# Keys 0 to 383 by threes in 128 partitions, a separate tile of tails, one k and one v load per pair of heads, six score buffers, a new order

## The chip, the cores and the metric

The kernel runs on one core of a Trainium2 chip. The metric is the device time of one execution in microseconds; the profile is of one execution of its own. The engines are TensorE (PE; PEld is its weight load), VectorE (DVE), ScalarE (ACT), GpSimd (POOL) and SyncE (SP), which issues most transfers. ACT issues some as well, in line with its calculations.

## The reference

Attention with mixed heads, for 4 batches, 12 heads, 448 positions and 64 values per head, then a gated network over the 768 joined values:

```
scores = (q @ k.T) / 8;  scores = sum over h of scores[h] * w_pre[h, g]
e = exp(scores - rowmax); a = e / (sum(e) + 1e-9)
a = sum over h of a[h] * w_post[h, g];  x = a @ v          (heads side by side)
h = relu(x @ w_in); c = 3-tap convolution of h along the positions
out = (h * sigmoid(c)) @ w_out
```

## The kernel before

A batch's 448 query rows are cut into four chunks, so there are 16 chunks c of 100 to 120 rows. Chunk c runs through these steps. `k_load`/`k_tr`/`k_out` and `q_load`/`q_tr`/`q_out` bring keys and queries and turn them on PE (tiles `tk`, `tq`; `pre` holds batch 0's keys, `nkr` later ones), `qk` makes the scores of two heads (tile `s`), and `qk_out` copies each head to a score buffer (`st`, or `stx` and `pre` at the start). `relayout` is a transfer of one head from its rows into `mt`, where ten query rows and twelve heads share the partitions, so that `premix` (tile `m`) mixes heads by one matmul. `premix` of a chunk needs all twelve re-layouts of it. Then `row_max` (VectorE), `row_exp` (ScalarE), the sums, and `postmix`, which mixes heads again and turns the result into two accumulators `t`; `post_out` copies them to `at`, one on ScalarE and one on VectorE, and only then can the next pair of tiles use them. `av` multiplies by v (tile `a`), `av_out` and `av_add` write x on ScalarE and VectorE.

The network is interleaved. Its weights come as 64-bit numbers and are decoded: `dec_load` (tile `raw`, two buffers), then five `dec_step`s, of which the first is ScalarE's (L354). `mm1` makes h, which goes out and comes back with a border for `conv`, `gate`, `glu`, and `mm2` makes the output rows.

Nothing is scheduled at run time. Each engine runs its instructions in the order in which the program emits them, and that order is the table `PLACES`: for each kind of step a list of places in one common order, which `plan` sorts. Transfers issued by SP stand in SP's queue in that order as well; a transfer that has to wait holds those behind it. Ahead of the plan, `FIRST` lists the first loads, alternately on SP and ACT.

The keys are not kept in their natural order along the 448 columns; any order does, as long as v has the same. Here partition j below 64 holds four neighbouring keys and partition j from 64 on holds three (JC = 4, TAIL = 64). So a pair of heads needs four k transfers (two per head: 64 partitions with four keys, 64 with three and a shared neighbour), and three v transfers (the four-key half, the three-key half, and a copy of each fourth key into the second half, so that both halves of the array have it). In batch 0 the two heads lie apart, with 1 KB per partition and head, and each key block is turned by one matmul per head.

Of the kernel before, what the change touches and what calls it, by code (L numbers as in the profile page):

```python
# [9 lines left out]
F32 = mybir.dt.float32  # L10
# [13 lines left out]
B, H, S, D = 4, 12, 448, 64  # L24
# [4 lines left out]
JC = 4  # L29
TAIL = 64  # L30
# [13 lines left out]
ST_X, ST = 12, 5  # L44
# [4 lines left out]
FIRST = [("q_load", 0, 0), ("k_load", 0, 0, 0), ("k_load", 0, 1, 0), ("k_load", 0, 2, 0), ("q_load", 0, 1), ("k_load", 0, 3, 0),  # L49
         ("k_load", 0, 4, 0), ("k_load", 0, 5, 0), ("q_load", 1, 0), ("q_load", 1, 1)]  # L50
# [8 lines left out]
def ring_slot(i):  # L59

    if i < 4 * H:
# [20 lines left out]
    qk_out=[14, 16, 28, 22, 23, 18, 37, 34, 40, 42, 49, 54, 53, 64, 58, 57, 63, 62, 68, 69, 74, 73, 127, 129, 137, 138,  # L82
# [9 lines left out]
    premix=[75, 80, 89, 93, 112, 166, 172, 181, 203, 205, 215, 306, 311, 325, 346, 348, 366, 418, 434, 444, 475, 495,  # L92
# [789 lines left out]
```

## Time and profile before

| | |
|---|---|
| three runs, median (lowest to highest) | 637.31 us (634.23 to 641.98) |
| the profiled execution, its own time | 641.89 us |
| its span, first to last instruction | 640.1 us |
| granted TensorE clock, mean | 0.981 |
| PE busy, weight loads busy | 592.9 us (93%), 477.2 us (75%) |
| VectorE, ScalarE, GpSimd busy | 439.1, 401.2, 78.0 us |
| transfers | 98.37 MB, mean 154 GB/s |

The attention of the 16 chunks ends at about 489 us, with the network's first product beside it; the rest is the network alone. A share of busy time is a mean over both.

### The profile page before, as it was taken

Reading aid. Unit: us, or ns where it says so; the run is one execution under the profiler, and the core shown is the slowest. Engines: PE = TensorE matmul, PEld = TensorE weight load, DVE = VectorE, ACT = ScalarE, POOL = GpSimd, SP = SyncE. Lnnn points to the kernel's source line nnn. Section 1 sums busy time; section 2 is a strip of 40 time slices with the busy share of each in tenths; the row PEclk is TensorE's granted clock in tenths of the full one; section 3 lists DMA queues with packets and bytes.
Section 4 is the critical chain, followed back from the end, with each engine's and each line's share of the span. In section 5 each row is a group of like instructions: output and inputs, shape, how many; then the busy total and the mean of one; then the engine's idle time right before and its main releaser. Section 6 shows DMA issues by size and latency. Waiting matters only on the chain.

```text
span 640.1 us, 26197 instructions
## 1 busy us (share of the span) xinstructions
PE 592.9 (93%) x11113; PEld 477.2 (75%) x11113; DVE 439.1 (69%) x1172; ACT 401.2 (63%) x1082; POOL 78.0 (12%) x165
## 2 busy tenths in 40 slices
PE   6987799999799999889999999999978999999997
PEld 4455676676667777667776876768768999999997
DVE  2564486687767678477666686857877999876721
ACT  1485686787678687687767688768757754232310
POOL 8001010011122112010111101121100000000000
PEclk8997998999989999999999999999997999999999
DMA  7565664776566665564566566555543324333211
GB/s 180 163 186 164 187 185 109 214 183 177 157 189 188 183 184 164 170 173 137 168 186 183 168 173 212 167 167 157 167 150 92 112 59 149 106 90 120 80 75 74
DMA packets 106708, 98.37 MB, mean 154 GB/s; under 512 B 56940, under 2 KB 97760, under 8 KB 106592
## 3 DMA queue, kind: packets, MB, share of 16 engines
q1 hardware_dynamic: 103628, 94.18, 50.8%
q10 hardware_dynamic: 2868, 2.52, 1.4%
q8 instruction: 87, 1.43, 0.9%
q14 instruction: 29, 0.24, 0.1%
q0 software_dynamic: 96, 0.01, 0.0%
HBM read 41.98 MB, written 15.99 MB: 91 GB/s over the span
## 4 chain that ended last, share of the span: by engine, by line
PE 70%; DMA 9%; issue 6%; DVE 5%; ACT 4%; SPq 3%; ACTq 1%; POOL 1%; POOLq 0%
PE o L816 18%; PE h L724 14%; PE m L543 9%; PE a L643 9%; PE t L587 8%; PE s L507 8%; DMA mt<-st 2%; DMA raw<-in_moe_w_in_dram 2%; DVE nm L548 2%; PE tq L484 1%; PE tk L463 1%; DMA v<-in_v_dram 1%; DMA raw<-in_moe_w_out_dram 1%; DMA pre<-in_k_dram 1%; DVE at L372 1%
## 5 line engine op out<-in xcount | busy, mean ns | idle before, releaser
L587 PEld LDWEIGHTS t<-wn,e 60*64 60x64 f32 x5040 | 104.4, 135 | 44.6 <-issue 28.4
L724 PE MATMUL h<-xp,lp 128*128 128x448 f32 x576 | 132.5, 377 | 5.4 <-ACT x L653 3.7
L556 ACT ACTIVATE e<-m,nm 124x448 f32<-124x448 f32 x180 | 113.7, 637 | 35.3 <-DVE nm L548 28.7
L548 DVE TENSOR_REDUCE nm<-m 124x1 f32<-124x448 f32 x180 | 106.6, 618 | 30.7 <-PE m L543 28.7
L724 PEld LDWEIGHTS h<-xp,lp 128*128 128x128 f32 x576 | 105.0, 189 | 23.2 <-ACT x L653 5.3
L816 PE MATMUL o<-wo,g 128*128 128x384 f32 x672 | 118.9, 337 | 0.0
L587 PE MATMUL t<-wn,e 60*64 60x60 f32 x5040 | 108.4, 221 | 10.7 <-issue 6.9
L816 PEld LDWEIGHTS o<-wo,g 128*128 128x128 f32 x672 | 117.7, 188 | 0.3
L543 PE MATMUL m<-mt,wpre 64*64 64x448 f32 (+1 forms) x704 | 91.9, 559 | 11.5 <-DMA v<-in_v_dram 4.8
L370 ACT COPY st<-s 120x448 f32<-120x448 f32 (+2 forms) x154 | 78.9, 543 | 30.5 <-DMA mt<-st 15.7
L507 PE MATMUL s<-mk,mq 64*64 64x448 f32 (+3 forms) x768 | 94.0, 547 | 2.6 <-ACT mk L370 2.5
L643 PEld LDWEIGHTS a<-at,v 64*64 64x64 f32 x3072 | 79.2, 138 | 22.3 <-issue 12.2
L643 PE MATMUL a<-at,v 64*64 64x120 f32 (+5 forms) x3072 | 85.5, 254 | 7.3 <-issue 3.4
L372 DVE COPY at<-t 128x420 f32<-128x420 f32 (+2 forms) x96 | 54.3, 565 | 37.9 <-PE t L587 34.6
L714 DVE TENSOR_TENSOR lp<-wi,lp 128x128 fp32r<-128x128 f32 x192 | 51.9, 289 | 20.7 <-ACT lp L710 20.5
L710 ACT CAST lp<-wi 128x128 fp32r<-128x128 f32 x192 | 54.7, 305 | 8.8 <-PE h L724 8.5
L562 POOL TENSOR_SCALAR sm<-sm 124x2 f32<-124x2 f32 (+1 forms) x92 | 22.5, 245 | 299.8 <-ACT e L556 279.0
L370 ACT COPY at<-t 128x420 f32<-128x420 f32 (+2 forms) x96 | 51.6, 543 | 9.7 <-PE t L587 9.2
L543 PEld LDWEIGHTS m<-mt,wpre 64*64 64x64 f32 (+1 forms) x704 | 30.2, 135 | 31.8 <-issue 17.4
L356 POOL TENSOR_SCALAR dw<-dw 128x256 f32<-128x256 f32 x48 | 41.4, 864 | 97.1 <-ACT dw L354 91.2
L507 PEld LDWEIGHTS s<-mk,mq 64*64 64x64 f32 (+3 forms) x768 | 29.5, 127 | 21.9 <-issue 10.8
L785 DVE SCALAR_TENSOR_TENSOR cv<-hpad,cws,cv 128x448 f32<-128x448 f32 x64 | 42.5, 680 | 1.0
(71 smaller groups left out, 501.1 us busy)
## 6 DMA issues: line engine op xcount, KB each, us to landing
mt<-st SPq DMA_DIRECT2D x82, 210.0 KB
h<-hs SPq DMA_DIRECT2D x32, 224.0 KB
hpad<-h SPq DMA_DIRECT2D x32, 224.0 KB
mt<-st SPq DMA_DIRECT2D x36, 192.5 KB
mt<-st SPq DMA_DIRECT2D x36, 175.0 KB
raw<-in_moe_w_in_dram SPq DMA_DIRECT2D x24, 256.0 KB
raw<-in_moe_w_out_dram SPq DMA_DIRECT2D x24, 256.0 KB
nqr<-in_q_dram SPq DMA_DIRECT2D x31, 192.0 KB
```

Of the source, the lines that this page charges most:

```text
L370: nc.scalar.copy(out=out, in_=in_)
L372: nc.vector.tensor_copy(out=out, in_=in_)
L507: nc.tensor.matmul(out=pqs[c, h - 1 + i][m:e], lhsT=qops[c][s, p, o + m:o + e], rhs=kops[b, p][s], start=True, stop=True)
L543: nc.tensor.matmul(out=pms[c, some[i]][64 * s:64 * s + 64], lhsT=wpre[rows, i], rhs=mt[rows, some[s]], start=True, stop=True)
L548: nc.vector.tensor_reduce(out=nm[0:PN], in_=pms[c, t][0:PN], axis=AX.X, op=ALU.max, negate=True)
L556: nc.scalar.activation(out=e[0:PN], in_=pms.pop((c, t))[0:PN], func=AF.Exp, bias=nm[0:PN], accum_out=sums[c, t // 2][0:PN, t % 2:t % 2 + 1])
L587: nc.tensor.matmul(out=pts[c, k][s][64 * half:64 * half + 64, block], lhsT=e[rows, o:o + 64], rhs=wn[rows, i], start=True, stop=True)
L643: nc.tensor.matmul(out=out, lhsT=vts[b, p][rows, hh, (j + 1) % JC], rhs=rhs, start=(j == 3 and p % 3 == 0), stop=(j == 2), skip_group_chec ...
L710: nc.scalar.copy(out=lps[b, f, kk][:, 0], in_=wi[:, kk, f * 128:(f + 1) * 128])
L714: nc.vector.tensor_tensor(out=t[:, 1], in0=wi[:, kk, f * 128:(f + 1) * 128], in1=t[:, 0].bitcast(F32), op=ALU.subtract)
L724: nc.tensor.matmul(out=phs[b, f], lhsT=w, rhs=x, start=(kk + j == 0), stop=(kk == KC - 1 and j == 2))
L816: nc.tensor.matmul(out=pos[r, o], lhsT=g, rhs=w, start=(f == 0 and j == 0), stop=(f == FC - 1 and j == 2))
```

## The change

Keys 0 to 383 lie by threes in 128 partitions (JC = 3, JM = 384). The 64 tails, keys 384 to 447, lie in a tile of their own: for k one of 64 partitions by 6 heads in each half (`kt`, one buffer), for v one with all twelve heads in both halves (`vtail`). `k_load` and `load_v` are one transfer per pair of heads; `k_tail` and `v_tail` are two per batch. `k_tr` is four transposes per pair in every batch, of which the first turns the tails of pairs p and p + 3 (its other half is overwritten). In batch 0 a key is now a piece of 256 bytes on both sides, as before in the others. A score pool has six buffers instead of five.

```
-JC = 4
-TAIL = 64
+JC, JM = 3, 384
-ST_X, ST = 12, 5
+ST_X, ST = 12, 6
-FIRST = [("q_load", 0, 0), ("k_load", 0, 0, 0), ("k_load", 0, 1, 0), ("k_load", 0, 2, 0), ("q_load", 0, 1), ("k_load", 0, 3, 0),
-         ("k_load", 0, 4, 0), ("k_load", 0, 5, 0), ("q_load", 1, 0), ("q_load", 1, 1)]
+FIRST = [("q_load", 0, 0), ("k_tail", 0, 0), ("k_load", 0, 0), ("k_tail", 0, 1), ("k_load", 0, 1), ("k_load", 0, 2), ("q_load", 0, 1),
+         ("k_load", 0, 3), ("k_load", 0, 4), ("k_load", 0, 5), ("q_load", 1, 0), ("q_load", 1, 1)]
...
+    v_tail=[148, 161, 753, 754, 1492, 1459, 2205, 2295],
...
+    kt_p = pool("kt", 1)
...
-    def k_load(b, p, hh, eng=nc.sync):
...
-        for h in (0, 1) if b == 0 else (hh,):
-            first = k[b, 2 * p + h]
-            eng.dma_start(out=x[0:TAIL, h], in_=first[0:JC * TAIL].rearrange("(j c) d -> j c d", c=JC))
-            rows = bass.AP(first.tensor, first[JC * TAIL - 1].offset, [[(JC - 1) * D, 128 - TAIL], [1, JC * D]])
-            eng.dma_start(out=x[TAIL:128, h], in_=rows.rearrange("j (c d) -> j c d", c=JC))
+    def tails_of(x, b, h0, h1):
+
+        return x[b, h0:h1, JM:S].rearrange("h j d -> j h d")
+
+    def k_load(b, p, eng=nc.sync):
+
+        nat["k", b, p] = nat["k0"][:, p] if b == 0 else nk_p.tile([128, JC, 2, D], F32, tag="nk", name="nkr")
+        eng.dma_start(out=nat["k", b, p], in_=k[b, 2 * p:2 * p + 2, 0:JM].rearrange("h (j c) d -> j c h d", c=JC))
+
+    def k_tail(b, i, eng=nc.sync):
+
+        if i == 0:
+            nat["kt", b] = kt_p.tile([128, H // 2, D], F32, tag="kt", name="kt")
+        eng.dma_start(out=nat["kt", b][64 * i:64 * i + 64], in_=tails_of(k, b, 6 * i, 6 * i + 6))
 
     def k_tr(b, p):
+
         pl, tag = (ps_m, "m") if b else (ps_t, "t") if p % 3 < 2 else (ps_a, "a")
-        trs["k", b, p] = pl.tile([128, JC, 128], F32, tag=tag, name="tk")
-        x = nat.pop(("k", b, p))
+        trs["k", b, p] = to = pl.tile([128, 512], F32, tag=tag, name="tk")
+        x, q, o = nat.pop(("k", b, p)), p % 3, JM - 64 * (p // 3)
+        nc.tensor.transpose(out=to[:, o:o + 128], in_=nat["kt", b][:, 2 * q:2 * q + 2].rearrange("j h d -> j (h d)"),
+                            identity=ident)
         for c in range(JC):
-            to = trs["k", b, p][:, (c - 1) % JC]
-            if b:
-                nc.tensor.transpose(out=to, in_=x[:, :, c].rearrange("j h d -> j (h d)"), identity=ident)
-                continue
-            for hh in range(2):
-                nc.tensor.matmul(out=to[64 * hh:64 * hh + 64], lhsT=x[:, hh, c], rhs=ident, start=True, stop=True)
+            nc.tensor.transpose(out=to[:, 128 * c:128 * c + 128], in_=x[:, c].rearrange("j h d -> j (h d)"), identity=ident)
...
     def load_v(b, p):
-        vts[b, p] = vall[:, p]
-        x = v[b, 2 * p:2 * p + 2]
-        lo = x[:, 0:JC * TAIL].rearrange("h (j c) d -> j h c d", c=JC)
-        nc.sync.dma_start(out=vts[b, p][0:TAIL].rearrange("j h c d -> j h (c d)"),
-                          in_=lo.rearrange("j h c d -> j h (c d)"))
-        nc.sync.dma_start(out=vts[b, p][TAIL:128, :, 1:JC].rearrange("j h c d -> j h (c d)"),
-                          in_=x[:, JC * TAIL:S].rearrange("h (j c) d -> j h (c d)", c=JC - 1))
-        nc.sync.dma_start(out=vts[b, p][TAIL:128, :, 0], in_=lo[:, :, 0])
+
+        nc.sync.dma_start(out=vmain[:, p].rearrange("j h c d -> j h (c d)"), in_=v[b, 2 * p:2 * p + 2, 0:JM].rearrange("h (j c) d -> j h (c d)", c=JC))
+
+    def v_tail(b, i):
+
+        nc.sync.dma_start(out=vtail[64 * i:64 * i + 64], in_=tails_of(v, b, 0, H))
...
-                    nc.tensor.matmul(out=out, lhsT=vts[b, p][rows, hh, (j + 1) % JC], rhs=rhs, start=(j == 3 and p % 3 == 0),
-                                     stop=(j == 2), skip_group_check=True)
+                    nc.tensor.matmul(out=out, lhsT=v_j, rhs=rhs, start=(j == JC and p % 3 == 0),
+                                     stop=(j == JC - 1), skip_group_check=True)
```

`postmix`, `post_out` and `av` are written for the new constants, with the same shapes. All of `PLACES` is new, for the network's steps too. Some of its places, and the PE steps that stand in the list between the two:

| the last `relayout` of a chunk, its first `premix` | before | after |
|---|---|---|
| chunk 1 | 165, 166: none | 133, 171: 1 premix, 4 postmix, 2 qk |
| chunk 3 | 400, 418: 1 qk, 2 postmix | 390, 425: 6 postmix, 1 k_tr, 3 qk |
| chunk 13 | 2278, 2280: none | 2253, 2294: 2 mm1, 2 qk, 2 postmix |
| chunk 14 | 2487, 2489: none | 2475, 2500: 3 postmix, 3 av, 2 qk |
| chunk 15 | 2599, 2635: 4 postmix, 2 premix, 3 av | 2652, 2653: none |

The later `v_tail` of batch 2 has place 1492, the last `av` of batch 1 has 1455 and the first of batch 2 has 1525, with four postmix and two premix between the last two. The last store of the output is of row group 12, in one transfer; it was of group 13, in two halves.

## Rows read from the trace of the kernel before

**Rows 1.** The page: busy time by engine; the chain that ended last.

```profile
PE 592.9 (93%) x11113; PEld 477.2 (75%) x11113; DVE 439.1 (69%) x1172; ACT 401.2 (63%) x1082; POOL 78.0 (12%) x165
...
PE 70%; DMA 9%; issue 6%; DVE 5%; ACT 4%; SPq 3%; ACTq 1%; POOL 1%; POOLq 0%
```

**Rows 2.** Windows: stretch, length, busy by engine, clock, DMA share, GB/s.

```profile
20.00:40.00 20.00, 18.57 (x252) 8.35 (x244) 13.90 (x32) 12.09 (x31) 0.81 (x4) 1.00 0.63 185
...
520.00:560.00 40.00, 40.00 (x226) 39.49 (x225) 36.33 (x72) 16.06 (x35) 0.00 (x0) 1.00 0.36 113
```

**Rows 3.** Timeline, 0 to 16 us: start, length, engine, line, operation [idle before].

```profile
0.81 0.61 ACTq L452 DMA_DIRECT2D pre<-in_k_dram  x1
...
5.66 0.59 SPq L478 DMA_DIRECT2D nqr<-in_q_dram  x1
...
9.16 0.90 PE L484 MATMUL tq<-ident,nqr 128*128 128x128 f32 x3 [3.49 <-DMA nqr<-in_q_dram]
...
12.94 1.28 ACT L414 ACT_TABLE_LOAD   x1 [12.94 <-DMA pre<-in_k_dram]
...
15.29 2.58 PE L507 MATMUL s<-mk,mq 64*64 64x448 f32 x24 [1.39 <-ACT mk L370]
```

**Rows 4.** Timeline, 42 to 54 us.

```profile
42.99 3.53 SPq L523 DMA_DIRECT2D mt<-stx  x4
...
46.57 0.97 SPq L617 DMA_DIRECT2D v<-in_v_dram  x1
...
51.58 3.27 PE L543 MATMUL m<-mt,wpre 64*64 64x448 f32 x16 [4.83 <-DMA v<-in_v_dram]
```

**Rows 5.** Timeline of PE alone, 90 to 460 us: the waits spoken of.

```profile
97.48 1.76 PE L543 MATMUL m<-mt,wpre 64*64 64x448 f32 x8 [1.66 <-DMA nkr<-in_k_dram]
...
176.44 1.49 PE L724 MATMUL h<-xp,lp 128*128 128x448 f32 x3 [3.72 <-ACT x L653]
...
398.46 0.98 PE L543 MATMUL m<-mt,wpre 64*64 64x448 f32 x8 [1.11 <-DMA mt<-st]
...
453.10 1.74 PE L543 MATMUL m<-mt,wpre 64*64 64x448 f32 x16 [0.79 <-DMA mt<-st]
```

**Rows 6.** Timeline, 163 to 178 us: SP's queue and ScalarE.

```profile
163.68 1.47 SPq L617 DMA_DIRECT2D v<-in_v_dram  x1
...
167.15 1.40 SPq L454 DMA_DIRECT2D nkr<-in_k_dram  x1
...
171.09 0.45 SPq L692 DMA_DIRECT2D raw<-in_moe_w_in_dram  x1
...
175.61 0.43 ACT L354 ACTIVATE dw<-raw 128x256 f32<-128x256 f32 x1 [1.96 <-DMA raw<-in_moe_w_in_dram]
```

**Rows 7.** Windows at the lower clock, columns as in rows 2.

```profile
51.50:56.50 5.00, 4.92 (x68) 3.08 (x72) 2.73 (x7) 2.23 (x7) 0.21 (x1) 0.50 0.58 166
97.00:101.00 4.00, 3.52 (x37) 1.77 (x41) 1.16 (x2) 0.96 (x3) 0.00 (x0) 0.57 0.67 177
176.00:180.00 4.00, 3.56 (x16) 2.93 (x20) 1.40 (x6) 2.50 (x8) 1.07 (x2) 0.57 0.72 235
```

**Rows 8.** One line's instructions, L452: duration in ns, least, median, most.

```profile
L452 SPq DMA_DIRECT2D nkr<-in_k_dram x36: 544/602/1767, 12.2 to 345.1; - x36
```

**Rows 9.** Groups by line and shape: turning keys of batches 1 to 3.

```profile
L463 PE MATMUL tk<-ident,nkr 128*128 128x128 f32 x72 | 11.2, 278 | 0.2
```

**Rows 10.** Timeline, 0 to 32 us: turning one pair of batch 0.

```profile
22.62 1.09 PE L466 MATMUL tk<-ident,pre 128*64 128x128 f32 x16
```

**Rows 11.** The chain in order of time: start, length, what.

```profile
2.09 3.39 DMA pre<-in_k_dram
...
92.11 5.31 DMA nkr<-in_k_dram
```

**Rows 12.** Timeline of PE alone, 30 to 480 us: two waits ahead of postmix.

```profile
40.27 1.08 PE L587 MATMUL t<-wn,e 60*64 60x60 f32 x55 [0.18 <-ACT at L370]
...
473.77 0.85 PE L587 MATMUL t<-wn,e 60*64 60x60 f32 x42 [2.25 <-issue]
```

More of the change, by code (lines that the diff above doesn't have):

```diff
@@ L264 @@
[L264 to L265 removed]
+    q_tr=[0, 9, 38, 59, 80, 92, 76, 198, 387, 463, 516, 560, 555, 588, 895, 886, 1010, 960, 1243, 1227, 1237, 1231,
+        1627, 1721, 1844, 1912, 2044, 1997, 2241, 2193, 2439, 2501],
+    q_load=[4, 19, 18, 149, 274, 430, 452, 494, 482, 499, 793, 808, 813, 941, 1087, 1165, 961, 1097, 1330, 1560, 1670,
+        1863, 1743, 1807, 2078, 2136, 1951, 2265],
+    k_tr=[5, 6, 2, 14, 36, 20, 327, 324, 395, 443, 466, 515, 735, 924, 1005, 1125, 1175, 1182, 1553, 1724, 1856, 1858,
+        1926, 2037],
@@ new lines @@
+    k_load=[243, 8, 366, 397, 432, 462, 677, 794, 963, 954, 1127, 1149, 1242, 1360, 1569, 1728, 1862, 1880],
+    k_tail=[233, 248, 573, 668, 1255, 1298],
+    v_tail=[148, 161, 753, 754, 1492, 1459, 2205, 2295],
+    qk=[11, 12, 31, 26, 44, 40, 48, 61, 68, 65, 78, 73, 82, 90, 85, 120, 146, 160, 245, 262, 282, 286, 297, 304, 416,
[4 rows of a table added]
+    qk_out=[17, 23, 46, 13, 33, 32, 29, 27, 45, 49, 41, 42, 57, 51, 66, 62, 69, 70, 67, 72, 79, 88, 75, 74, 83, 95, 91,
[9 rows of a table added]
+    premix=[96, 100, 114, 135, 130, 171, 175, 197, 221, 241, 209, 306, 315, 338, 341, 369, 388, 425, 440, 457, 489,
[4 rows of a table added]
@@ new lines @@
+    row_max=[97, 98, 101, 102, 117, 116, 138, 136, 131, 164, 172, 176, 193, 205, 208, 214, 222, 224, 255, 254, 210,
[9 rows of a table added]
+    sum_eps=[109, 112, 137, 166, 177, 185, 217, 232, 238, 278, 279, 321, 330, 364, 375, 410, 411, 455, 447, 510, 519,
[4 rows of a table added]
+    postmix=[119, 126, 140, 141, 155, 156, 173, 174, 183, 187, 211, 215, 226, 227, 251, 258, 275, 276, 292, 294, 301,
[9 rows of a table added]
+    post_out=[127, 128, 142, 147, 163, 168, 179, 178, 192, 196, 223, 216, 242, 234, 260, 271, 277, 281, 295, 299, 303,
[9 rows of a table added]
+    av=[230, 231, 256, 267, 268, 269, 314, 318, 320, 345, 351, 352, 448, 449, 467, 508, 533, 534, 591, 592, 593, 614,
[4 rows of a table added]
@@ new lines @@
+    av_out=[257, 272, 333, 353, 468, 535, 602, 617, 836, 873, 1080, 1102, 1271, 1301, 1415, 1458, 1535, 1619, 1824,
+        1881, 2065, 2094, 2123, 2167, 2425, 2488, 2589, 2625, 2748, 2763, 2789, 2809],
+    av_add=[261, 293, 336, 361, 484, 536, 605, 620, 837, 928, 1093, 1108, 1279, 1332, 1419, 1486, 1576, 1620, 1828,
+        1882, 2080, 2095, 2140, 2169, 2426, 2489, 2599, 2630, 2786, 2792, 2795, 2810],
+    load_cw=[514, 566, 746],
+    emit_cw=[790],
+    net_init=[2573],
+    room=[213],
+    dec_load=[16, 200, 244, 354, 402, 470, 547, 633, 597, 752, 806, 839, 911, 952, 984, 1008, 1047, 1067, 1119, 1147,
+        1198, 1190, 1267, 1305, 1337, 1354, 1416, 1454, 1558, 1636, 1600, 1731, 1667, 1779, 1840, 1886, 1913, 1986,
+        2003, 2165, 2131, 2272, 2264, 2334, 2395, 2421, 2493, 2495],
@@ new lines @@
+    relu=[728, 815, 938, 1023, 1161, 1239, 1369, 1517, 1578, 1693, 1732, 1794, 1855, 1948, 2015, 2051, 2225, 2296,
+        2347, 2405, 2474, 2531, 2695, 2732, 2894, 2890, 2922, 2972, 2956, 3048, 3041, 3135],
+    conv=[2650, 2651, 2697, 2723, 2784, 2791, 2729, 2754, 2774, 2839, 2852, 2853, 2862, 2863, 2885, 2913, 2914, 2927,
[5 rows of a table added]
+    wo_load=[2659, 2660, 2661, 2745, 2750, 2817, 2891, 2935],
+    mm2=[2944, 3012, 2987, 3042, 2967, 3038, 2943, 3045, 3058, 3059, 3046, 3060, 3071, 3134, 3072, 3151, 3122, 3129,
+        3108, 3127, 3168, 3169, 3214, 3244, 3163, 3164, 3159, 3166, 3193, 3275, 3270, 3289, 3233, 3261, 3266, 3267,
+        3189, 3265, 3242, 3243, 3276, 3278, 3286, 3287, 3283, 3285, 3293, 3295, 3284, 3288, 3307, 3309, 3271, 3300,
+        3303, 3304],
@@ new lines @@
+    mm2_out=[3013, 3043, 3139, 3140, 3084, 3085, 3175, 3192, 3144, 3150, 3202, 3245, 3204, 3205, 3298, 3299, 3263,
+        3268, 3279, 3280, 3282, 3291, 3294, 3296, 3308, 3310, 3301, 3305],
+    store=[3044, 3170, 3113, 3201, 3180, 3256, 3290, 3302, 3269, 3281, 3292, 3297, 3311, 3306],
+    q_out=[1, 25, 39, 60, 81, 93, 77, 199, 398, 464, 517, 576, 561, 589, 906, 892, 1011, 970, 1245, 1240, 1244, 1233,
+        1637, 1741, 1853, 1943, 2071, 2013, 2269, 2209, 2462, 2502],
+    k_out=[7, 10, 3, 15, 37, 21, 329, 326, 400, 450, 471, 518, 743, 935, 1016, 1148, 1176, 1183, 1561, 1738, 1867,
+        1860, 1928, 2053],
@@ L266 @@
+    wo_hi=[2692, 2727, 2782, 2751, 2804, 2854, 2983, 2954],
+    wo_lo=[2721, 2728, 2790, 2772, 2988, 2883, 3001, 2978],
 )
@@ L276, in indices @@
     some = dict(
-        q_tr=grid(NCH, 2), q_load=grid(range(2, NCH), 2), k_tr=grid(B, NP), k_load=grid(range(1, B), NP, 2),
+        q_tr=grid(NCH, 2), q_load=grid(range(2, NCH), 2), k_tr=grid(B, NP), k_load=grid(range(1, B), NP), k_tail=grid(range(1, B), 2), v_tail=grid(B, 2),
         qk=grid(NCH, range(1, H, 2)), qk_out=grid(NCH, H), premix=pairs, row_max=tiles, sum_eps=pairs,
@@ L435, in keep_busy @@
             nc.tensor.matmul(out=ps, lhsT=zero[:, 0:128], rhs=zero[:, 0:S], start=True, stop=True)
-    def keys(x, h):
-        lo, hi = x[h, 0:JC * TAIL], x[h, JC * TAIL:S]
-        return lo.rearrange("(j c) d -> j c d", c=JC), hi.rearrange("(j c) d -> j c d", c=JC - 1)
-    def k_load(b, p, hh, eng=nc.sync):
-        if ("k", b, p) not in nat:
-            nat["k", b, p] = (nat["k0"][:, p] if b == 0 else
-                              nk_p.tile([128, JC, 2, D], F32, tag="nk", name="nkr").rearrange("j c h d -> j h c d"))
-        x = nat["k", b, p]
-        for h in (0, 1) if b == 0 else (hh,):
-            first = k[b, 2 * p + h]
-            eng.dma_start(out=x[0:TAIL, h], in_=first[0:JC * TAIL].rearrange("(j c) d -> j c d", c=JC))
-            rows = bass.AP(first.tensor, first[JC * TAIL - 1].offset, [[(JC - 1) * D, 128 - TAIL], [1, JC * D]])
-            eng.dma_start(out=x[TAIL:128, h], in_=rows.rearrange("j (c d) -> j c d", c=JC))
+    def tails_of(x, b, h0, h1):
+        return x[b, h0:h1, JM:S].rearrange("h j d -> j h d")
@@ L468, in k_out @@
     def k_out(b, p):
         kops[b, p] = ko[:, (NP * b + p) % 7]
-        copy_of(("ACT", "DVE")[p % 2], kops[b, p], trs.pop(("k", b, p)).rearrange("p c j -> p (c j)")[:, 0:S])
+        copy_of(("ACT", "DVE")[p % 2], kops[b, p], trs.pop(("k", b, p))[:, 0:S])
     def q_load(c, g, eng=nc.sync):
@@ L577, in postmix @@
         if i == 0:
-            pts[c, k] = [ps_t.tile([128, 2 * JC - 1, 60], F32, tag="t", name="t") for s in range(2)]
+            pts[c, k] = [ps_t.tile([128, 2 * JC + 1, 60], F32, tag="t", name="t") for s in range(2)]
         e, wn = es.pop((c, 2 * k + i)), wns[c, k]
-        pieces = [(3 * i + j, half, 128 * j + 64 * half) for j in range(JC - 1) for half in range(2)]
-        pieces.insert(6 * i, (2 * JC - 2, i, S - TAIL))
+        pieces = [(3 * i + j, half, 128 * j + 64 * half) for j in range(JC) for half in range(2)]
+        pieces.insert(6 * i, (2 * JC, i, JM))
         for block, half, o in pieces:
@@ L584, in postmix @@
                 rows = slice(64 * s, 64 * s + 12 * HR)
-                if o == S - TAIL and len(PAIRS[c][k]) == 1:
+                if o == JM and len(PAIRS[c][k]) == 1:
                     half = s
@@ L595, in post_out @@
         if not ats:
-            ats["all"] = at_p.tile([128, 2 * JC - 1, 12, 90], F32, tag="at", name="at")
+            ats["all"] = at_p.tile([128, 2 * JC + 1, 12, 90], F32, tag="at", name="at")
         pair = len(PAIRS[c][k]) == 2
@@ L628, in av @@
             pas[c] = [pl.tile([128, 3, 128], F32, tag=tag, name="a") for pl, tag in ((ps_a, "a"), (ps_m, "m"))]
-        for j in (3, 0, 1, 2):
+        for j in (JC, 0, 1, 2):
             for hh in range(2):
                 for i in range(2):
-                    blocks = slice(j, j + JC, JC - 1) if j < 3 else slice(6, 7)
+                    blocks = slice(j, j + JC + 1, JC) if j < JC else slice(2 * JC, 2 * JC + 1)
                     rows = slice(64 * i, 64 * i + 64)
@@ L635, in av @@
                     out = pas[c][i][64 * hh:64 * hh + 64, p % 3].rearrange("d (b x) -> d b x", b=2)
-                    if j == 3:
+                    v_j = vmain[rows, p, hh, j] if j < JC else vtail[rows, 2 * p + hh]
+                    if j == JC:
                         out = out[:, i:i + 1]
@@ L831, in tile_talking_heads_conv_glu @@
     emit = {f.__name__: f for f in (
-        k_load, k_tr, k_out, q_load, q_tr, q_out, qk, qk_out, relayout, premix, row_max,
-        row_exp, sum_eps, sum_rec, post_w, postmix, post_out, load_v, av, av_out, av_add, x_hi, x_lo, w_hi, w_lo, load_cw, emit_cw,
+        k_load, k_tail, k_tr, k_out, q_load, q_tr, q_out, qk, qk_out, relayout, premix, row_max,
+        row_exp, sum_eps, sum_rec, post_w, postmix, post_out, load_v, v_tail, av, av_out, av_add, x_hi, x_lo, w_hi, w_lo, load_cw, emit_cw,
         dec_load, dec_step, dec_store, mm1, relu, store_h, wo_load, wo_hi, wo_lo, net_init, room, load_h, conv, gate,
```

110 lines of the change are left out of this document (34 added, 76 removed), and 250 rows, old and new, of tables (av, conv, dec_step, mm1).

## The prediction

> **What bounds the kernel now.** I read the page's busy times and the chain of waits first [rows 1]: TensorE (PE) is busy for 592.9 of 640.1 us and the chain runs through it for 70%, with 9% in transfers. So time can go only where PE stands idle (47.2 us in all), where its clock is halved, or where it has less to do. The windows say where not to look: from 520 us on PE is full, 40.00 of 40 us [rows 2]. The order is new there too, but PE has no idle time to give back, and I count nothing there but the last store. What is left is the start and the attention stage.
>
> The timeline of the start shows the largest single loss. The first score matmul begins at 15.29 us, 14 us after the first load was issued [rows 3]. Two things hold it. The second half of q, the sixth load in SP's list, is issued at 5.66 and frees PE at 9.16. And ScalarE, which has to copy the first transposed keys, is busy as an issuer: 17 loads stand ahead of its first calculation, which starts at 12.94. The second loss is at 46.75 us, where PE stops for 4.83 us ahead of the first premix of chunk 1 [rows 4]. The trace names a v load, but this matmul reads no v: it reads the re-laid scores, whose last four transfers SP issued up to 46.52, and 5.1 us later PE goes on. Such waits come back, shorter, at 97.48, 398.46 and 453.10, all ahead of the first premix of a chunk (3, 13 and 15), and 3.72 us at 176.44 [rows 5]. That last one is indirect [rows 6]: SP issues v and k loads from 163.68 and a weight piece only at 171.09; ScalarE stands at the decode of that piece until 175.61, and its copy of x, which PE waits for, is queued behind. After each of the longer stops the granted clock is at the lower level, 0.50 for 51.5 to 56.5 us [rows 7].
>
> **What the change does, part by part.** *Issues.* The list of loads falls from 96 for k and 72 for v to 32 and 32, tails included: 104 fewer on SP and ACT, at 0.602 us of queue each [rows 8] 63 us of queue time. SP isn't on the path as such, so this is worth nothing by itself; it counts where PE waits for something that SP issued late.
>
> *The start.* ACT now has six loads ahead of its first calculation instead of 17. At the 0.71 us each of before ((12.94 - 0.81)/17, [rows 3]) it is free at about 5.1 us and, after the 1.28 us of table load, at 6.4. The second half of q is SP's fourth load, not its sixth. So the first score matmul can come at 8 to 10 us. Keys of batch 0 are turned by four transposes per pair (0.156 us each, 11.2/72, [rows 9]) instead of a group of 1.09 us [rows 10]: 0.47 us less for each of six pairs, 2.8 us of PE work. If nothing else held PE, it would be at the premix of chunk 1 at 46.75 - 6.3 (start at 9.0) - 1.8 (three transposes and the list's difference) = 38.7 us instead of 51.58, a gain of 12.9. But the data have to come. Ahead of the last re-layout of chunk 1 the list of before moves 8.64 MB (counted from the tiles: q 1.38, k 1.70, decode 0.52, v 0.52, scores 4.52), that of after 7.92 MB. At the pace of before (8.64 MB by 51.58 us, 168 GB/s) they are there at 47.3 us; at the 185 GB/s of 20 to 40 us [rows 2] at 42.8 and the landing after it. I take 44.5, a gain of 7.1, less 0.7 us because the new list has done less other PE work there (one score group and one q turn more, four half postmixes fewer): **-6.4**, between -12.2 and -3.6.
>
> Batch 0's keys came in pieces of 1 KB and now come in pieces of 256 bytes, as the later batches' do: those landed in 5.31 us, the first ones in 3.39 [rows 11]. The Trainium skill ("DMA: Bandwidth & Descriptors", Why small descriptors are slow) speaks against this part: a 256-byte piece takes 11 cycles of which 8 carry data, by the same count a 1 KB one 35 of which 32 do, so a byte takes a quarter longer. By an estimate from that page 1.38 MB, 7.4 us at 185 GB/s, would take 1.9 us longer and this part would give -4.5.
>
> *The clock behind the stop.* 5.0 us at half clock cost 2.5 us of work [rows 7]. Whether PE stops long enough again is open: **-1.0** (-2.5 to 0).
>
> *Waits for re-laid scores.* From the last re-layout in the list to the first premix the old list has no PE work at all for chunks 1, 13 and 14, and 2.0 us for chunk 3; the new one has 4.9, 4.2, 5.6 and 6.5 (PE steps between the two places, at their durations in the timeline). The waits of chunks 3 and 13, 1.66 and 1.11 us, and the 4 us at clock 0.57 behind the first of them, 1.7 us [rows 5, 7], make 4.5: **-3.0** (-4.5 to 0).
>
> *ScalarE behind weight pieces.* 3.72 us and 1.7 us of clock [rows 5, 7]. In the new list one of 48 pieces has its decode step less than 1 us of PE work behind its load, in the old one eight; and in the stretch above three v and two k issues, of up to 1.47 us, stand ahead of the late piece [rows 6], where the new form has one of each. **-3.2** (-5.4 to 0).
>
> *What is new and costs.* (a) Chunk 15's last re-layout now stands directly ahead of its premix; it had 6.1 us. That distance cost chunk 14 nothing, chunk 13 1.11 and chunk 1 4.83 us: +1.0 (0 to 7.3 with the clock). (b) One v tail serves all heads, so it waits for the last value matmul of a batch, and the next batch's first one waits for it; SP's later loads are queued behind that wait. The tightest is batch 2's, with 4.0 us of PE work between, against 0.6 to issue and 5.31 to land: +0.8 (0 to 3.6). k tails have 9 us or more. (c) Both accumulators of postmix are taken by a pair of tiles, and nine hand-overs from pair to pair now have under 1 us of PE work between, in the old list two. At one of those two PE waits 0.18 us; the longest wait ahead of a postmix group, with no releaser named, is 2.25 [rows 12]. Seven more at 0.25 are +1.8 (1.3 to 15.8). (d) The last store is now a whole row group, 0.2 MB more: +0.5 (0 to 1.1 at 185 GB/s). The sixth score buffer lets ScalarE copy one head further ahead; its gain is in the waits above, and it can't cost PE time.
>
> Sum: -6.4 - 1.0 - 3.0 - 3.2 + 1.0 + 0.8 + 1.8 + 0.5 = **-9.5 us**. The profiled execution took 641.89 us, so it would take 632.4; that execution is near the slowest of the runs, and taken off their median of 637.31 the sum gives **627.8**.
>
> **The rivals.** *A, transfers set the start and stay as slow.* For it: the share of the DMA engines is already 0.58 to 0.72 in the windows of the start and of these waits [rows 2, 7]. Then scores arrive at 47.3 us, the clock falls again, and later waits give a third: -3.6 - 1.0 - 1.6 + 4.1 = -2.1, so 635.2. Against it: there are stretches at 235 GB/s [rows 7]. The skill (the same page, Why a DMA increments its semaphore by 16 and not by 1) would make this likelier: a transfer uses the largest count up to 16 that divides both outer sizes, and a re-layout has ten rows on one side, so ten engines carry all of them; no view here separates the engines. *B, slower: the accumulator of postmix.* If ScalarE and VectorE, which empty it, are behind when PE comes back after one group, each of the seven new short hand-overs costs what the worst row shows, 15.8 us in all instead of 1.8, and two stops grow long enough to halve the clock, 1.7 each: -9.5 + 14.0 + 3.4 = +7.9, so 645.2. It decides from about 1.6 us each on (11.3/7: then the gain is gone). Against it, the short one of before costs 0.18. *C, PE sets the start.* All four gains at their far ends and costs at the near ones, -12.2 - 2.5 - 4.5 - 5.4 + 1.3 = -23.3: 614.0. *D, the queue was hidden anyway* leaves the start's -6.4, which comes from ScalarE, and pays the four costs: -6.4 + 4.1 = -2.3, so 635.0, counted with A.
>
> **How the numbers follow.** Forecast 0.48, A with D 0.27, C 0.15, B 0.10. The range takes in C's end, A and D, and about half of the way from D to B: 614 to 640. About 1% (6.4 us) is what a measurement of this kernel can tell from no change, its three runs spread by 1.2%. Faster by over 1%, below 630.9: C, nine tenths of the forecast's width and a little of A, 0.61. Slower by over 1%, above 643.7: most of B, 0.09. Within: 0.30.
>
> **What would show it.** In the new trace: first score matmul near 9 us, ScalarE's first calculation near 5; PE at the premix of chunk 1 at 44 to 45; no stop of over 1.7 us at 97 and 176; PE idle down to about 38 us. Wrong if the first premix of chunk 1 still comes at 47 or later with PE standing (A), if the waits ahead of postmix groups grow by over 10 us (B), or if the stage after the attention, which I leave as it is, has idle time.

## The result, and the profile after

The changed kernel took 631.0 us (median of 20 runs, 625.45 to 637.97) beside 637.57 us for the kernel before (20 runs, 634.23 to 643.97). The ratio is 0.9882, 95% interval 0.9857 to 0.9908: 6.6 us faster by the medians, where 9.5 were forecast. The profiled execution took 629.37 us with a span of 627.7, against 641.89 and 640.1; so the two profiles lie 12.4 us apart, 1.9 times the difference of the medians, and what follows from their rows is to be read against 12.4. A ratio leaves out every run that is over 1.5% above the fastest of its kernel (four of these 20 for the changed kernel), while a median is of all runs.

The page of the kernel after: busy time by engine, transfers, the queue that brings instructions (packets, MB, share), and the chain that ended last.

```profile
PE 589.2 (94%) x11041; PEld 466.3 (74%) x11041; DVE 438.1 (70%) x1172; ACT 403.5 (64%) x1084; POOL 78.4 (12%) x165
...
DMA packets 109651, 97.57 MB, mean 155 GB/s; under 512 B 61420, under 2 KB 100704, under 8 KB 109536
...
q8 instruction: 87, 1.43, 1.0%
...
PE 82%; DMA 6%; issue 4%; DVE 4%; ACT 2%; ACTq 1%; POOL 0%; SPq 0%; DVEq 0%
```

Beside [rows 1] PE's idle time falls from 47.2 to 38.5 us and its busy time by 3.7; the chain runs through PE for 82% in place of 70%, and transfers fall from 9% to 6%. The windows, with the columns of [rows 2], cut after's span where the first premix of chunk 1 starts and where the attention ends; the same cuts of before, at 51.58 and 490, follow.

```profile
0.00:47.86 47.86, 37.75 (x407) 18.45 (x410) 22.96 (x47) 22.36 (x52) 15.70 (x29) 0.93 0.80 188
47.86:478.00 430.14, 406.07 (x9827) 305.20 (x9820) 311.27 (x914) 326.27 (x903) 62.67 (x136) 0.99 0.63 172
478.00:627.70 149.70, 145.38 (x814) 142.67 (x812) 103.90 (x213) 54.90 (x131) 0.00 (x0) 1.00 0.29 97
```

```profile
0.00:51.58 51.58, 38.80 (x579) 23.22 (x580) 23.75 (x51) 23.97 (x56) 14.98 (x29) 0.95 0.64 177
51.58:490.00 438.42, 407.69 (x9722) 310.72 (x9723) 309.88 (x905) 320.42 (x894) 63.05 (x136) 0.98 0.60 169
490.00:640.10 150.10, 146.41 (x814) 143.27 (x812) 105.49 (x217) 56.80 (x133) 0.00 (x0) 1.00 0.31 101
```

The first lengths say where the 12.4 us are: 3.7 in the start, 8.3 in the rest of the attention, 0.4 in the network.

The start, to be read beside [rows 3] and [rows 4], is in two timelines of after: of all engines, and of PE alone.

```profile
0.82 1.42 ACTq L453 DMA_DIRECT2D kt<-in_k_dram  x2
2.27 2.63 ACTq L447 DMA_DIRECT2D pre<-in_k_dram  x3
...
6.40 1.14 ACTq L475 DMA_DIRECT2D nqr<-in_q_dram  x1
...
7.57 1.28 ACT L415 ACT_TABLE_LOAD   x1 [7.57 <-issue]
...
10.53 1.75 PE L504 MATMUL s<-mk,mq 64*64 64x448 f32 x8
...
20.26 1.26 ACTq L520 DMA_DIRECT2D mt<-pre  x1
...
21.62 2.75 ACTq L520 DMA_DIRECT2D mt<-pre  x2
...
25.69 0.59 PE L504 MATMUL s<-mk,mq 64*64 64x448 f32 x4 [3.24 <-ACT mq L371]
```

```profile
47.86 1.00 PE L540 MATMUL m<-mt,wpre 64*64 64x448 f32 x8
...
61.31 0.47 PE L641 MATMUL a<-at,v 64*64 64x100 f32 x9 [1.90 <-issue]
...
69.24 1.12 PE L641 MATMUL a<-at,v 64*64 64x50 f32 x21 [3.59 <-issue]
```

The first score matmul comes 4.8 us earlier, but the first premix of chunk 1 only 3.7: on the way there is a new stop of 3.24 us, where PE waits for a copy of ScalarE, and ScalarE is issuing re-layouts. The 4.83 us ahead of the premix itself are gone. Two stops with no releaser stand behind it. What premix waited for from 90 to 480 us, the answer to [rows 5], is a line of the view of PE by tile:

```profile
its engine sat idle before it (us, times) until:
  issue: 2.6, 2
```

No premix of chunks 3 to 15 waits for a transfer any more, and by the same view of `h` no product of the network waits for ScalarE's copy of x. The windows of [rows 7] at 97 and 176 us now have the full clock:

```profile
97.00:101.00 4.00, 3.84 (x129) 2.42 (x124) 2.56 (x7) 3.75 (x11) 0.22 (x1) 1.00 0.60 149
176.00:180.00 4.00, 4.00 (x81) 3.01 (x83) 1.54 (x6) 2.47 (x9) 0.22 (x1) 1.00 0.67 201
```

### The profile page after: what moved, and what is told of

Its sections match the earlier page's. It is cut to its first block, busy times and chain, and to the rows that moved or that the text cites. A ratio compares the mean times of both kernels' runs of the same rounds, so it can differ in the third digit from the quotient of the medians.

```text
span 627.7 us, 25923 instructions
## 1 busy us (share of the span) xinstructions
PE 589.2 (94%) x11041; PEld 466.3 (74%) x11041; DVE 438.1 (70%) x1172; ACT 403.5 (64%) x1084; POOL 78.4 (12%) x165
## 4 chain that ended last, share of the span: by engine, by line
PE 82%; DMA 6%; issue 4%; DVE 4%; ACT 2%; ACTq 1%; POOL 0%; SPq 0%; DVEq 0%
PE o L814 19%; PE h L722 18%; PE t L584 12%; PE a L641 10%; PE m L540 10%; PE s L504 10%; PE tq L481 2%; DMA mt<-st 1%; DMA raw<-in_moe_w_in_dram 1%; DVE nm L545 1%; DMA pre<-in_k_dram 1%; PE tk L463 1%; DMA v<-in_v_dram 1%; DVE at L373 1%; DMA w_out_s<-dw 1%
## 5 line engine op out<-in xcount | busy, mean ns | idle before, releaser
L584 PEld LDWEIGHTS t<-wn,e 60*64 60x64 f32 x5040 | 101.0, 135 | 48.0 <-issue 28.2
L584 PE MATMUL t<-wn,e 60*64 60x60 f32 x5040 | 106.9, 221 | 10.7 <-issue 7.4
L540 PE MATMUL m<-mt,wpre 64*64 64x448 f32 (+1 forms) x704 | 88.8, 544 | 3.3 <-issue 2.6
L786 ACT ACTIVATE cv<-cv 128x448 f32<-128x448 f32 x32 | 18.2, 578 | 43.9 <-DVE cv L783 43.9
```

The source lines that it names most:

```text
L540: nc.tensor.matmul(out=pms[c, some[i]][64 * s:64 * s + 64], lhsT=wpre[rows, i], rhs=mt[rows, some[s]], start=True, stop=True)
L584: nc.tensor.matmul(out=pts[c, k][s][64 * half:64 * half + 64, block], lhsT=e[rows, o:o + 64], rhs=wn[rows, i], start=True, stop=True)
```

## The experiments

In the table, ratios are to the kernel before on the same chip, with their 95% intervals. There are four groups, timed apart from each other: the changed kernel, x1 to x4, x5 to x8, and x9 to x12. Ratios compare less well across them than inside one.

| kernel | loads and tiles | order | score buffers | chunk 0's re-layouts issued by | median us | ratio |
|---|---|---|---|---|---|---|
| changed kernel | new | new | 6 | SP and ACT | 631.0 | 0.9882 (0.9857 to 0.9908) |
| x1_layout | new | old | 5 | SP and ACT | 635.55 | 0.9900 (0.9826 to 0.9975) |
| x5_old_order_six | new | old | 6 | SP and ACT | 630.41 | 0.9909 (0.9870 to 0.9948) |
| x2_order | old | new | 5 | SP and ACT | 665.39 | 1.0432 (1.0351 to 1.0513) |
| x4_five_buffers | new | new | 5 | SP and ACT | 642.96 | 1.0117 (1.0034 to 1.0199) |
| x3_sp_relayouts | new | new | 6 | SP | 624.35 | 0.9792 (0.9725 to 0.9859) |
| x12_sp_again | new | new | 6 | SP | 624.32 | 0.9790 (0.9707 to 0.9873) |
| x9_old_order_six_sp | new | old | 6 | SP | 630.0 | 0.9828 (0.9761 to 0.9895) |

**The parts alone.** My theory was that the distances in the new list took the waits away; the rival was that 104 fewer issues did, by shortening the queue.

x1_layout is the changed kernel in the order of before, with five buffers; its `PLACES` are those of before, one place for each k load, and tails next to the loads.

```
-ST_X, ST = 12, 6
+ST_X, ST = 12, 5
-PLACES = dict(...)   # after
+PLACES = dict(...)   # before
```

> The new layout and loads in the old order of steps, five score buffers (tails put ahead of their first reader, 16 to 30 PE steps or more). Theory O, the distances in the new list took the waits away: only the start gets shorter, by about 3 us (ScalarE free earlier, 2.8 us less turning), the stop ahead of the first premix of chunk 1 and the ones near 97 and 176 us stay: 633 to 636. Rival Q, the 104 issues taken out of the queue did it: most of the gain is there, 630 to 633, and the stops near 97 and 176 us are under 1 us.

It came to 0.9900, as Q wanted, but that ratio rests on three runs, one of them at 624.38 us and the next at 633.43; the median of all ten, 635.55, is 0.998 of before's 636.88 and lies in O's range. The stops are divided as well: the ones ahead of chunks 1 and 3 stay (6.97 and 1.69 us), and the one of 3.72 us at 176 is gone. So x1_layout decides nothing by itself. x2_order is the other half: the kernel before, whose code stays, with the places of after (both k loads of a pair at the pair's place, no tails).

```
-PLACES = dict(...)   # before
+PLACES = dict(...)   # after
```

> The old layout with all its 168 loads in the new order of steps, five score buffers. Theory O: the waits for re-laid scores and the one behind a weight piece are gone as in the changed kernel, the start is as slow as before: 632 to 635. Rival Q: with the old queue the late loads stay late, 636 or more, and PE waits for transfers as before.

It was 4.3% slower, 28.5 us by the medians. So the new order with the old loads and five buffers is no gain at all. x4_five_buffers asks for the part that the prediction gave no price:

```
-ST_X, ST = 12, 6
+ST_X, ST = 12, 5
```

> The changed kernel with five score buffers instead of six. Both theories put no gain on the sixth buffer: 630 to 632. If it carries some, ScalarE waits for buffers near premixes and the time is 634 or more.

One buffer less costs 12 us by the medians (642.96 against 631.0, ratios 1.0117 and 0.9882). The list of waits shows how (who waits, for whom: us in sum, times, longest); first x4_five_buffers, then the kernel before, after and x2_order.

```profile
ACT st L371 <- DMA mt<-st: 27.0, 19, 3.7
```

```profile
ACT st L370 <- DMA mt<-st: 15.7, 14, 2.4
```

```profile
ACT st L371 <- DMA mt<-st: 1.8, 4, 0.6
```

```profile
ACT st L220 <- DMA mt<-st: 44.2, 21, 7.2
```

ScalarE's copy of a score waits until a re-layout has emptied the buffer. The new order asks for scores earlier, so with five buffers this wait grows to 27.0 us, and to 44.2 with the old loads, and everything behind it in ScalarE's line comes late; with six, in after, it is 1.8 us. x5_old_order_six asks whether the sixth buffer helps the old order as well:

```
-PLACES = dict(...)   # after
+PLACES = dict(...)   # before
```

> The new layout and loads with the order of before, as in x1_layout, but with the sixth score buffer. Theory S (the sixth buffer pays only where the order asks for scores further ahead, as the new one does): ratio to before 0.985 to 0.992, within 0.4% of x1_layout's 0.9900, and ScalarE's waits for free score buffers, 9.4 us in x1_layout, fall while PE's stops at 46, 96 and 397 us stay. Rival S2 (the sixth buffer pays in any order): 0.971 to 0.980, as the new order gained 12 us from it (1.0117 to 0.9882), and the three stops go. If S holds, the new order with six is worth what separates this run from 0.9882.

0.9909 lies in the range of theory S and outside S2's, and the waits are as S has them: ScalarE's 9.4 us for free buffers are gone from the list, and PE's stops stay. How many microseconds the sixth buffer is worth in the old order is not shown, since the ratio of x1_layout is so loose (medians 0.998 of before's there and 0.988 here). PE's stop ahead of chunk 1's premix stays, as in [rows 4]; the timeline of PE in x5_old_order_six:

```profile
51.69 3.26 PE L391 MATMUL m<-mt,wpre 64*64 64x448 f32 x15 [5.28 <-DMA mt<-stx]
```

One stop of before is gone here without the new order: no product of the network waits for ScalarE's copy of x at 176 us, and the window of 170 to 180 us of x5_old_order_six has the full clock, where before had 0.57 over 176 to 180 [rows 7].

```profile
170.00:180.00 10.00, 9.81 (x259) 7.27 (x252) 7.78 (x25) 7.79 (x22) 1.29 (x3) 1.00 0.77 217
```

So layout, loads and sixth buffer give 0.9% in the old order, and layout and loads take 3% off the new order with five buffers (1.0432 to 1.0117). What the new order adds where both sides have six buffers is less clear. By 0.9909 and 0.9882 it is 0.3%, with intervals that overlap. But three kernels in the new order that were timed beside x5_old_order_six, each one small edit away from the changed kernel, came to 0.9807, 0.9815 and 0.9839 (x7_768_bytes, x6_shift and x8_later_loads, below), and beside those it is 0.7% to 1.0%, with intervals that overlap a little.

**ScalarE as an issuer.** x3_sp_relayouts takes chunk 0's six re-layouts from ScalarE:

```
-        (nc.sync if c or h % 2 else nc.scalar).dma_start(out=nat["mt"]...
+        nc.sync.dma_start(out=nat["mt"]...
```

> The changed kernel with all re-layouts of chunk 0 issued by SP, none by ScalarE. If ScalarE as an issuer makes the 3.24 us stop at 22.45 us (it needs 2.75 us for two issues there), the stop goes and the time falls by 2 to 4 us, 627 to 629. If the transfers themselves are late (the DMA engines are busy for 0.99 of the first 20 us), SP's longer queue takes back what ScalarE gains: 630 to 633.

It is the fastest kernel of the study, 0.9792, below both expected ranges, and again 0.9790 as x12_sp_again: 6.7 us below the changed kernel by the medians. The changed kernel was not timed beside it, and its near copies x6_shift, x7_768_bytes and x8_later_loads lie between the two, so how much of the 0.9% is this edit's stays open; the first premix is what the traces show. The timeline of PE in x3_sp_relayouts has chunk 1's first premix at 43.41 us in place of 47.86, and the stop of 3.24 us is gone:

```profile
43.41 0.98 PE L540 MATMUL m<-mt,wpre 64*64 64x448 f32 x8 [0.19 <-DMA mt<-st]
...
69.62 0.59 PE L584 MATMUL t<-wn,e 60*64 60x60 f32 x12 [6.30 <-issue]
```

The windows behind that stop, after first and then x3_sp_relayouts, show that the clock was part of its price:

```profile
26.00:31.00 5.00, 5.00 (x35) 1.67 (x27) 2.34 (x4) 1.68 (x4) 0.00 (x0) 0.66 0.66 207
```

```profile
26.00:31.00 5.00, 3.59 (x33) 1.52 (x35) 1.09 (x2) 3.13 (x8) 0.00 (x0) 1.00 0.62 208
```

0.66 in place of 1.00 over 5 us is 1.7 us, and with the stop 4.9; the premix came 4.45 us earlier. The instructions of the re-layout line on ScalarE's queue (ns: least, median, most), after and before:

```profile
L520 ACTq DMA_DIRECT2D mt<-pre x6: 780/1195/1422, 12.9 to 23.1; - x6
```

```profile
L523 ACTq DMA_DIRECT2D mt<-pre x6: 771/780/1420, 16.9 to 26.1; - x6
```

The median of the same six issues is now half as long again. One by one, the first three are alike (1.42, 0.81 and 0.78 us in both). The last three take 0.77 or 0.78 us in before, where 0.6 us or more lie between one and the next, and 1.26 and twice 1.37 us in after, where each follows soon upon the other, from 20.26 to 24.37 us. The share of the DMA engines was high then (0.86 for 12.9 to 24.4 us), but that doesn't explain it: in x7_768_bytes below it was 0.68 over the six issues, and the last two took longer still. Why they are long stays open.

```profile
21.73 3.33 ACTq L528 DMA_DIRECT2D mt<-pre  x2
```

x12_sp_again is the same kernel once more, beside x9_old_order_six_sp, which has the same one line in the kernel of x5_old_order_six.

> The same kernel as x3_sp_relayouts, on the chip and in the rounds of x9_old_order_six_sp, so that the two orders can be compared with the rest alike: 0.976 to 0.983 by both theories, 622 to 627 us.

> New layout, six score buffers and all re-layouts issued by SP, as in x3_sp_relayouts, but in the order of before. Theory P (the order itself is worth what its stops are, some 11 us of PE's idle time between x5_old_order_six and the changed kernel): 1.0% or more slower than x12_sp_again, ratio 0.985 to 0.993 to before. Rival P0 (what the new order saves in stops it gives back elsewhere: x5_old_order_six came to 0.9909 and the changed kernel to 0.9882): within 0.5% of x12_sp_again, ratio 0.976 to 0.984. PE's stops at 46, 94 and 392 us should stay by both, since they are of the order.

0.9828 for the old order and 0.9790 for the new: 0.4% apart with overlapping intervals, which is P0's side; by the medians of all runs, 630.0 and 624.32, it is 0.9%, nearly P's. So neither is settled. All three comparisons of the orders have the same sign, from 0.3% to 1.0%, and none is clear of its intervals.

**The stops without a releaser.** PE's waits put down to "issue" ahead of postmix, premix and value groups grew from 11.3 us before (6.9, 3.4 and 1.0) to 18.2 after (7.4, 8.2 and 2.6). They lie in the middle of groups, and beside each there is a packet of the instruction queue: 66.5 to 67.8 us for the stop from 65.65 to 69.24. There are 87 such packets of 16 KB and 22,082 matmuls and weight loads, so one packet brings some 250 instructions, about 127 matmuls with their loads. In all 14 such stops of over 0.4 us in after, PE goes on 1.25 to 1.86 us after the end of the last packet before (counted from the trace). If PE waits for its own instructions (F), stops must lie at fixed numbers of the instruction, whatever work is there; if value matmuls wait for v (V), at fixed places of the work. x6_shift puts 50 more matmuls ahead of everything:

```
-BUSY = 9
+BUSY = 59
...
-            nc.tensor.matmul(out=ps, lhsT=zero[:, 0:128], rhs=zero[:, 0:S], start=True, stop=True)
+            if i < 4:
+                nc.tensor.matmul(out=ps, lhsT=zero[:, 0:128], rhs=zero[:, 0:S], start=True, stop=True)
+            else:
+                nc.tensor.matmul(out=ps[0:16, 0:16], lhsT=zero[:, 0:16], rhs=zero[:, 0:16], start=True, stop=True)
```

> The changed kernel with 100 more PE instructions in the work that fills the wait at the start (50 more matmuls of 16x16 and their weight loads, five big ones fewer), so that every later block of 256 PE instructions begins 100 instructions earlier in the work. Theory F (PE stops for its own next instructions): the stops of 1.90 us at 59.4 and 3.59 us at 65.7 leave their places in the work; they come some 3 us earlier, or at other sizes, each by a packet of the instruction queue, and not ahead of the same attention matmuls. Rival V (the attention matmuls wait for v): both stay ahead of the same L641 groups with 1.5 to 4 us. Time by both 628 to 634 us, ratio 0.984 to 0.993.

Counted from the traces: matmuls ahead of a stop, how many of them write a tile named `t...` (postmix and transposes) and how many `a` (times v), and the length of the stop.

```
kernel            matmuls   t...   a      stop us
after                 721    440    54     1.90
after                 848    496   101     3.59
x6_shift              848    468    87     3.98
x6_shift              976    496   179     1.34
x7_768_bytes          976    550   175     4.78
x8_later_loads        976    533   192     2.19
x3_sp_relayouts       976    533   192     6.30
x12_sp_again          976    533   192     2.21
after                9992   5191  2880     2.21
x6_shift             9993   5142  2880     2.54
```

721, 848 and 976 are 127 and 128 apart. In x6_shift the stop at 848 has 42 fewer matmuls of the two kinds ahead of it than in after, and the one at 9993 has 49 fewer `t`: the work has moved by the 50 matmuls, and the stops have kept their numbers. F holds; V falls. The time, 0.9815 (0.9740 to 0.9890), lies below the expected 0.984 to 0.993 and can't be told from after's.

Why the packet comes late is another question. x8_later_loads takes traffic away from there: five loads of SP go behind the last value matmul of chunk 0.

```
-k_tail(1,0) 233, k_load(1,0) 243, dec_load(2) 244, k_tail(1,1) 248, q_load(4,0) 274
+all five, in this order, behind av(0,5), place 269
```

> The changed kernel with five loads of SP (two key tails, one key load, one weight piece, one query load) issued behind the last attention matmul of chunk 0 in place of between 57 and 66 us. Theory F2 (instructions arrive late because the DMA engines are full): the DMA share of 60 to 66 us falls and the stop of 3.59 us at 65.7 falls under 1.5 us; 1 to 3 us gained, ratio 0.983 to 0.987. Rival F3 (the fetch has its own duration or PE waits for something else): a stop of 3 to 4 us stays there whatever the share; ratio 0.987 to 0.990. If the loads are then late for chunk 4's transposes, a wait shows at their L463 near 80 us.

The stop at 848 went, as F2 wanted, and one of 2.19 us came at 976:

```profile
71.03 0.40 PE L435 MATMUL t<-wn,e 60*64 60x60 f32 x12 [2.19 <-issue]
```

But the share that was to fall hardly did (60 to 66 us: 0.79 after, 0.76 here), and the time, 0.9839 (0.9760 to 0.9917), doesn't tell it from after. So F2 isn't shown. That the stop at 976 was 6.30 us in one trace of the SP kernel and 2.21 in the next, with shares of 0.97 and 0.86 in 60 to 66 us, speaks for full queues as the reason without showing it, and so do these slices of 55 to 70 us of x3_sp_relayouts (share of the DMA engines in tenths, 40 slices), in which the packet starts at 66.7 us, just when the engines empty:

```profile
DMA  6676679668667679999999999976788510000000
```

No view says which of the sixteen engines carried the packet and what stood ahead of it there; that stays open.

**The pieces of 256 bytes.** x7_768_bytes puts each head's three keys of a partition side by side in batch 0, one matmul per head in turning them:

```
-        nat["k0"] = pre[...].rearrange("p (n c h d) -> p n c h d", n=NP, h=2, c=JC)
+        nat["k0"] = pre[...].rearrange("p (n h c d) -> p n h c d", n=NP, h=2, c=JC)
...
+            for hh in range(2):
+                nc.tensor.matmul(out=to[64 * hh:64 * hh + 64, 128 * c:128 * c + 128], lhsT=x[:, c, hh], rhs=ident, ...)
```

> The changed kernel with batch 0's keys in pieces of 768 bytes in place of 256 (one row per head in the tile, so one matmul per head in place of one per pair when they are transposed, some 2 us more of PE at the start). Theory D (my term for the start came out small because pieces of 256 bytes fill the DMA engines): the DMA share of the first 20 us falls from 0.99 to under 0.93 and the first score matmul comes at 9.5 us or sooner in place of 10.53, the first premix of chunk 1 at 46.5 or sooner in place of 47.86; ratio 0.983 to 0.988. Rival E (ScalarE as issuer of re-layouts and the rest of the traffic set the start): share and first premix within 0.5 us of after, ratio 0.987 to 0.992.

The windows of the first 20 us, after and then x7_768_bytes:

```profile
0.00:20.00 20.00, 15.50 (x94) 8.78 (x98) 8.21 (x13) 5.51 (x10) 13.97 (x24) 0.91 0.99 190
```

```profile
0.00:20.00 20.00, 16.97 (x144) 10.16 (x144) 8.28 (x13) 5.69 (x10) 13.96 (x24) 1.00 0.88 192
```

The share falls by 0.11, 2.2 us of the engines' time. The prediction's estimate from the Trainium skill ("DMA: Bandwidth & Descriptors", Why small descriptors are slow) was 1.9 us, for 1.38 MB in pieces of 256 bytes instead of 1 KB; the same count gives an estimate of 1.4 for the 1.18 MB that are pieces of 768 bytes here. The trace agrees in the direction and roughly in the size. But the first score matmul came at 10.76 us and not sooner, and a stop of 3.60 us stayed where after has 3.24. The time was 0.9807 (0.9731 to 0.9882), beside 0.9815 and 0.9839 for x6_shift and x8_later_loads, which keep the pieces of 256 bytes. x10_sp_768 is the same kernel once more, in one execution: 633.13 us, beside a median of 639.48 for before, about 0.990.

> Not the kernel meant for this label: the changed kernel with batch 0's keys in 768-byte pieces once more, one look. It should repeat x7_768_bytes: a time of 622 to 629 us, the first score matmul near 10.8 us, and stops of PE after its matmuls 721, 849 and 977 in number, where its instructions come in blocks of 128 matmuls.

The time missed that range, and the first score matmul came at 14.16 us and not near 10.8; the stops held their numbers (721, 848 and 976). The share of its first 20 us was 0.78, so 2.2 us is no fixed figure of this kernel. A gain by the pieces is therefore not shown, and x11_sp_768_later, which joins x3, x7 and x8, adds nothing to x3: 625.01 us, 0.9799 (0.9695 to 0.9904).

> All that helped, together: re-layouts by SP, batch 0's keys in 768-byte pieces, five loads behind the attention matmuls of chunk 0. If the gains add up (0.9% by SP, 0.7% by the pieces, 0.4% by the loads): 0.968 to 0.972. If the pieces and the loads only moved instruction boundaries or lay within the spread of those runs: 0.975 to 0.982, within 0.4% of x12_sp_again.

## Why the prediction held, and where its steps did not

The direction and the range held; the reasons did so in part.

- **The start, -6.4: mis-sized, about -3.0.** The premix of chunk 1 moved by 3.7 us, less the 0.7 of work that the new list puts behind it. The forecast's 44.5 us could be reached: with all of chunk 0's re-layouts issued by SP it was 43.41. The step that failed is ScalarE's: I counted it as an issuer only up to its first calculation, at 0.71 us each. It was free at 7.57 us and not at 5.1: five issues took 0.81 us each, up to 4.90, and the sixth began only at 6.40 and took 1.14. And it was stopped again by two of chunk 0's re-layouts, 2.75 us, with PE waiting behind. The clock behind the old stop did come back, 2.5 us, and fell behind the new one, 1.7 us, so that term gave 0.8 net of its 1.0.
- **Waits for re-laid scores, -3.0, and ScalarE behind weight pieces, -3.2: the stops went.** 1.66, 1.11 and 0.79 us ahead of chunks 3, 13 and 15 and 3.72 us at 176.44 are not in after, nor are the half-clock windows behind them. The two terms have different causes: the stops ahead of chunks 3 and 13 stay in the old order and go with the new one, while the one at 176.44 is gone in x1_layout and x5_old_order_six too, so the new layout and loads took it away and not the distances. But "the sixth score buffer's gain is in the waits above" hid the condition: with five buffers the same list was 1.2% slower than before. PE steps between two places were the right measure for PE and left out what ScalarE needs to put the scores there in time.
- **104 issues "worth nothing by itself": wrong.** In the old order, with the stops ahead of chunks 1, 3 and 13 still there (5.28, 2.06 and 2.04 us in x5_old_order_six), the new layout and loads with six buffers give 0.9%; with the new order and five buffers layout and loads give 3%, which is clear of noise. That holds for layout and loads together. One row of it is the stop of 3.72 us at 176.44. But in x5_old_order_six PE's idle time (48.6 us) is no less than before's 47.2, of which its stops for instructions (below) are 18.5 us beside 11.3, and its busy time is 8.9 us less. No row holds the whole gain, and no run parted the issues from the turned keys. What the rest of it was stays open.
- **Costs.** (a) Chunk 15's premix and (b) the v tails: no wait of either in after, 0 for +1.0 and +0.8. (c) Postmix waits for its accumulators' copies 0.9 us after (ScalarE 0.6, VectorE 0.3) and 2.6 before (1.7 and 0.9): none of the +1.8, and rival B never showed. Its price was taken from a wrong row: the 2.25 us of [rows 12], with no releaser named, begins beside an instruction packet (471.4 to 472.3 us in before), and the next stop in before comes 128 matmuls later; it was no wait for an accumulator. (d) From PE's last matmul to the end of the span 4.28 us against 3.73: +0.55, as forecast.
- **Not in the sum:** the stops for instructions, 6.9 us more in the profile of after. The one from 65.65 us has the clock behind it too, by the window of after with the columns of [rows 2]:

```profile
69.24:74.00 4.76, 4.76 (x137) 4.75 (x140) 0.00 (x0) 0.84 (x2) 0.00 (x0) 0.50 0.21 46
```

3.59 us and half of 4.76 are 6.0. These stops differ from trace to trace of one kernel, so they are no fixed price of the change; but the one stop alone takes back most of what the waits of chunks 3, 13 and 15 and of ScalarE gave (7.3 us without their clock).
- **Rival A** was half right: its sign, a first premix of chunk 1 at 47 us or later, was there (47.86), and the DMA share of the first 20 us was 0.99 where before had 0.64. But the bytes did not set the time: with SP as issuer the same bytes gave 43.41. Its sum has a slip as well: a third of the later waits, 3.0 and 3.2, is 2.1 and not 1.6.

So a sum that came out 2.9 us from the medians was made of terms too large at the start, costs that didn't come, and a loss of which before had 11.3 us and whose row in [rows 12] was read as something else. That these nearly cancel, and that PE's idle time came out at 38.5 us where 38 were named, is luck and not a check of the terms.

## What to carry to other kernels

A new order and the buffers it draws on are one change: before counting waits that a list takes away, count how many buffers it holds at once and who waits when one is missing (27.0 us here). An issue is work of the engine that makes it, at the length that it has in its place (up to 1.4 us here, not 0.78); where PE waits for that engine, look for another to make it. A stop put down to "issue" in the middle of a group is read by counting instructions: if it keeps its number when work is put ahead of it, it is no wait for data.

## What the runs showed of the hardware that was not expected

- PE stood still for its own instructions, up to 6.30 us at a time and 18.2 us in all in after, at numbers 127 or 128 matmuls apart where a packet of the instruction queue came late; it went on 1.25 to 1.86 us after the packet's end. The stop at matmul 976 was 6.30 and 2.21 us in two traces of one kernel.
- ScalarE's issue of one re-layout took 0.77 or 0.78 us where the issues stood apart (before, the last three) and 1.26 to 1.37 us where they followed soon upon each other (after), with the same transfer.
- A stop of 3.24 us was followed by a granted clock of 0.66 over 26 to 31 us, and one of 3.59 us by 0.50 over 4.76 us.
